# Routing in two groups of tokens, weights' low parts on VectorE, later weight requests and a shorter general path, in a fused attention and mixture-of-experts kernel

## The chip, the cores and the metric

One core of a Trainium2 chip runs the program. The metric is the device time of one execution in microseconds; the kernel before is quoted by the median of its runs. The trace comes from one further, profiled execution.

## The reference

```python
def _attn_ref(q, k, v):                      # 2 batches, 8 heads, 768 tokens, width 64
    gamma = 1.0 - 2.0 ** (-5.0 - np.arange(H, dtype=np.float32))
    for t in range(S):
        state = gamma[None, :, None, None] * state + np.einsum('bhd,bhe->bhde', k[:, :, t], v[:, :, t])
        y[:, :, t] = scale * np.einsum('bhd,bhde->bhe', q[:, :, t], state)
...
def _moe_ref(x, w_gate, w1, w2, capacity):   # 1536 tokens, 8 experts, 512 -> 1024 -> 512
    logits = x @ w_gate
    expert_idx = np.argmax(logits, axis=1)
...
    for i in range(N):                       # a token's place is its rank within its expert
        e = expert_idx[i]
        if counts[e] < capacity:
            disp[e, counts[e]] = x[i]
...
    h = np.maximum(np.einsum('ecd,edf->ecf', disp, w1), 0.0)
    y = np.einsum('ecf,efd->ecd', h, w2)
...
        out[i] = gate_w[i] * y[expert_idx[i], pos[i]]
...
def _moe2_ref(x, w_in, w_out, a, b):         # 512 -> 2048 -> 512
    h = x @ w_in
    P = a[0] + a[1] * h + a[2] * h2 + a[3] * h3
    Q = 1.0 + np.abs(b[0]) * np.abs(h) + np.abs(b[1]) * h2
    return (P / (Q + 1e-06) @ w_out).astype(np.float32)
```

The three parts run one behind the other. The capacity is 384 tokens for each expert.

## The kernel before, in words

**Attention and routing** (`attention`, L539 to L637). The 1,536 tokens are twelve tiles of 128, numbered u, six for each batch. For each tile TensorE makes the scores (`scores`, line 328 as all of `mm`), the product with the running state (`inter`), the product with the values (`intra`), the new state (`state`), and one product that turns the tile and gives the gate's logits (`gate_mm`, L345). VectorE masks the scores (`mask`, L292) and scales the result (`attn_xt`, L334). GpSimd scales the values (`scale`, L264) and makes the tables of decay (`y_table`, L259). ScalarE copies the state, the logits and the rows (`gate_out`, L393), which go to a table `xd` in HBM.

Tokens are routed in groups of whole tiles, `GROUPS`; before these are 4, 3, 3 and 2 tiles. For a group VectorE finds the expert of each token (`gate_group`, L373 to L384), TensorE ranks the tokens within their experts (`rank_mm`, L410 to L420), VectorE turns ranks into slots (`rank_pos`, L444 to L455, and `rank_put`, L465 to L468), and TensorE puts the tokens' numbers into a table of slots (`place_mm`, L478), which VectorE adds up (L483). From the table come the indices (`indices`, L496) by which GpSimd gathers rows of `xd` (`fetch`, L792).

**Weights.** All products of the experts use each weight as a high and a low part. A half matrix (128x1024) is requested on SP's queue (`load_w`, L157); ScalarE makes its high part `whi` (`split_hi`, L143), then the low part `wlo` is a subtraction (`split_lo`, L148). During attention the tables `LOADS`, `HI_AT` and `LO_AT` say at which tile a half is requested and split; there the low part is GpSimd's work. From the expert stage on, `prep_next` splits on ScalarE and VectorE and keeps loads ahead.

**The tail and the first expert** (`attn_tail`, L652; `first_expert`, L750). Of expert 0, the first 128 tokens are known once the first seven tiles are placed. Their rows are gathered early (`early_gather`), turned (L644), and run through expert 0 (L686 for the first layer, 24 products; L714 for the second, 24) while the last tiles are still routed. All other gathers wait for the last group's indices. The first of them feeds L842.

**Experts 1 to 7 and the last layer** (`moe` from L854, `ffn`). Each expert is a run of products (L871 to L873, L898 to L900), and SP, ScalarE, VectorE and GpSimd prepare the next weights beside it.

**The general path** (`overflow`, L918). Behind expert 3 every engine reads a flag (L920) and branches (L925). When an expert has more tokens than its slots, a loop redoes all experts in a plain way; on these inputs the branch skips it. Every engine jumps over its own part of that code.

The order of the instructions on each engine is the order in which the code issues them.

## Time and profile before

| | us |
|---|---|
| median of 3 runs (531.73 to 534.88) | 533.1 |
| the profiled execution, its own time | 539.45 |
| its span in the trace | 537.7 |
| TensorE matmul busy, of the span | 509.7 (95%) |
| TensorE instructions in the trace | 3,540 matmuls, 3,540 weight loads |
| VectorE busy, of the span | 416.2 (77%) |
| mean granted TensorE clock | 0.985 |

PE is TensorE, PEld its weight loads, DVE VectorE, ACT ScalarE, POOL GpSimd, SP the queue that issues most transfers. A `q` behind an engine's name means its sequencer. Times in the trace are microseconds from the start of the span. Matmuls are pipelined, so a busy PE is not PE at its peak.

### The profile page before, as it was taken

How to read it: one execution, taken by the hardware profiler on the slowest of the kernel's cores; microseconds unless marked ns; L12 is line 12 of the kernel's file. 1: busy time of each engine (PE TensorE's matmuls, PEld its weight loads, DVE VectorE, ACT ScalarE, POOL GpSimd, SP SyncE). 2: the span in 40 equal slices, each digit the busy share in tenths (PEclk: the TensorE clock that was granted, in tenths of full speed). 3: DMA queues.
4: the chain of work that ended last, by engine and by line, in shares of the span. 5: the costliest groups of instructions: out<-in, count | busy, mean ns of one | idle time of the engine just before them, and what ended most of it. 6: DMA issues, size and time to landing. Idle time of an engine off the chain costs nothing.

```text
span 537.7 us, 9505 instructions
## 1 busy us (share of the span) xinstructions
PE 509.7 (95%) x3540; PEld 446.1 (83%) x3540; DVE 416.2 (77%) x644; ACT 361.4 (67%) x591; POOL 261.5 (49%) x195
## 2 busy tenths in 40 slices
PE   6989889999995899999999999999999999999994
PEld 3877767899995899999988888888888888888883
DVE  2479973887967387798569698999899998865972
ACT  1334423886674277685578899998999988676750
POOL 1676503124826164212035444776757765535765
PEclk9999989999999699999999999999999999999998
DMA  8998554689998589997610001230222200000103
GB/s 307 411 395 320 144 172 149 210 321 258 286 315 255 162 291 217 371 280 272 218 37 2 0 1 39 80 111 17 69 79 79 78 1 0 2 0 1 79 2 156
DMA packets 27123, 83.16 MB, mean 155 GB/s; under 512 B 4928, under 2 KB 5184, under 8 KB 27072
## 3 DMA queue, kind: packets, MB, share of 16 engines
q1 hardware_dynamic: 24448, 75.16, 42.9%
q0 software_dynamic: 2624, 7.35, 4.0%
q8 instruction: 29, 0.48, 0.3%
q14 instruction: 22, 0.18, 0.1%
HBM read 72.00 MB, written 10.49 MB: 153 GB/s over the span
## 4 chain that ended last, share of the span: by engine, by line
PE 73%; issue 4%; DVE 3%; DMA 3%; ACT 2%; POOL 2%; POOLq 0%; ACTq 0%; DVEq 0%
PE h L997 8%; PE h L999 8%; PE h L998 8%; PE o L1068 7%; PE o L1070 7%; PE o L1069 7%; PE l L871 4%; PE l L872 4%; PE l L873 4%; PE l L900 4%; PE l L899 4%; PE l L898 4%; PE l L714 2%; DMA wd<-gq 2%; PE l L686 2%
## 5 line engine op out<-in xcount | busy, mean ns | idle before, releaser
L148 DVE TENSOR_TENSOR wlo<-raw,whi 128x1024 fp32r<-128x1024 f32 x72 | 101.6, 1425 | 16.7 <-ACT whi L143 16.4
L1048 POOL TENSOR_TENSOR gg<-fx,gg 128x512 fp32r<-128x512 f32 x47 | 61.0, 1298 | 70.7 <-issue 62.5
L143 ACT ACTIVATE whi<-raw 128x1024 fp32r<-128x1024 f32 x80 | 83.1, 1053 | 3.5 <-PE l L899 2.1
L997 PE MATMUL h<-yh,whi 128*128 128x512 f32 x192 | 74.9, 390 | 0.4 <-DVE fx L1036 0.4
L1068 PE MATMUL o<-whi,gg 128*128 128x512 f32 x192 | 74.8, 390 | 0.0
L999 PE MATMUL h<-yh,wlo 128*128 128x512 f32 x192 | 74.8, 389 | 0.0
L998 PE MATMUL h<-yl,whi 128*128 128x512 f32 x192 | 74.7, 389 | 0.0
L1069 PE MATMUL o<-wlo,gg 128*128 128x512 f32 x192 | 74.7, 389 | 0.0
L1070 PE MATMUL o<-whi,gg 128*128 128x512 f32 x192 | 74.7, 389 | 0.0
L1023 POOL TENSOR_TENSOR fw<-fh,fw 128x512 f32<-128x512 f32 x48 | 64.3, 1340 | 20.8 <-ACT fw L1012 20.1
L871 PE MATMUL l<-xh,whi 128*128 128x224 f32 x224 | 63.5, 283 | 7.5 <-issue 7.5
L204 POOL TENSOR_TENSOR gq<-gq 128x512 int32<-128x512 int32 x16 | 25.2, 1575 | 92.7 <-DVE gq L201 67.9
L1010 ACT ACTIVATE fx<-h,ct 128x512 f32<-128x512 f32 x48 | 37.3, 777 | 39.4 <-PE h L999 37.8
L872 PE MATMUL l<-xl,whi 128*128 128x224 f32 x224 | 62.9, 281 | 0.0
L873 PE MATMUL l<-xh,wlo 128*128 128x224 f32 x224 | 62.8, 280 | 0.0
L898 PE MATMUL l<-hh,whi 128*128 128x224 f32 x224 | 61.9, 276 | 0.0
L900 PE MATMUL l<-hh,wlo 128*128 128x224 f32 x224 | 61.5, 274 | 0.0
L899 PE MATMUL l<-hl,whi 128*128 128x224 f32 x224 | 61.4, 274 | 0.0
L871 PEld LDWEIGHTS l<-xh,whi 128*128 128x128 f32 x224 | 44.4, 198 | 7.7 <-issue 7.7
L872 PEld LDWEIGHTS l<-xl,whi 128*128 128x128 f32 x224 | 44.4, 198 | 0.0
L873 PEld LDWEIGHTS l<-xh,wlo 128*128 128x128 f32 x224 | 44.4, 198 | 0.0
L1034 DVE SCALAR_TENSOR_TENSOR fw<-fw,cq,h 128x512 f32<-128x512 f32 x48 | 35.6, 742 | 10.0 <-ACT h L1029 10.0
(167 smaller groups left out, 1233.1 us busy)
## 6 DMA issues: line engine op xcount, KB each, us to landing
raw<-wm SPq DMA_DIRECT2D x64, 512.0 KB
r<-wf SPq DMA_DIRECT2D x32, 512.0 KB
kv<-kv SPq DMA_DIRECT2D x24, 512.0 KB
wd<-gq SPq DMA_DIRECT2D x16, 256.0 KB
raw<-wd SPq DMA_DIRECT2D x8, 512.0 KB
xd<-xs SPq DMA_DIRECT2D x12, 256.0 KB
ca<-ct SPq DMA_DIRECT2D x1, 384.0 KB
xg<-xd,gidx POOLq DMA_INDIRECT x16
```

The costliest lines, as they stand in the source:

```text
L143: nc.scalar.activation(out=self.whi[i][:, sl], in_=raw, func=AF.Copy)
L148: (eng or self.nc.vector).tensor_tensor(out=self.wlo[i][:, sl], in0=raw, in1=self.whi[i][:, sl].bitcast(F32), op=ALU.subtract)
L871: nc.tensor.matmul(ps[:, fi], lhsT=wh[:, sl], rhs=xh[:, k], start=(k == 0), stop=False)
L872: nc.tensor.matmul(ps[:, fi], lhsT=wh[:, sl], rhs=xl[:, k], start=False, stop=False)
L873: nc.tensor.matmul(ps[:, fi], lhsT=wl[:, sl], rhs=xh[:, k], start=False, stop=(k == 3))
L898: mm(lhsT=wh[:, ws], rhs=fh, start=(f == 0 and o % 2 == 0), stop=False)
L997: nc.tensor.matmul(h, lhsT=wh[:, sl], rhs=self.yh[:, k, ts], start=(k == 0), stop=False)
L998: nc.tensor.matmul(h, lhsT=wh[:, sl], rhs=self.yl[:, k, ts], start=False, stop=False)
L999: nc.tensor.matmul(h, lhsT=wl[:, sl], rhs=self.yh[:, k, ts], start=False, stop=(k == 3))
L1068: self.nc.tensor.matmul(ps, lhsT=gh[:, ms], rhs=wh[:, ws], start=first, stop=False)
L1069: self.nc.tensor.matmul(ps, lhsT=gh[:, ms], rhs=wl[:, ws], start=False, stop=False)
L1070: self.nc.tensor.matmul(ps, lhsT=gl[:, ms], rhs=wh[:, ws], start=False, stop=last)
```

## The change

Eight things are changed together.

1. **Groups**: two groups, tiles 0 to 6 and 7 to 11, in place of four.
2. **Low parts in attention on VectorE**, at other tiles: halves 0 to 3 within the loop, 4 and 5 in the tail, 6 and 7 in `first_expert`. The high parts are issued behind the gate's copies, also later. `LOADS` requests weights later.
3. **Order in the tail**: the last `gate_mm` is issued first, then `early_x` and sixteen of the products that need no low part of x, then the ranking. `first_expert` takes the second layer's products with the high part first.
4. **Start**: the decay table `t0` comes with the first transfer; the values of tile 0 are scaled on GpSimd, those of tile 1 on VectorE; the matrix of ones is set on the chip.
5. **Pairs of PSUM banks**: the two halves of scores and of results are one tile each, so `mask` and `attn_xt` are one instruction for each tile. The heads are laid out so that this works.
6. **PSUM pools**: attention has its own.
7. **Scatter of the row numbers** (`perm_put`): experts 4 to 7 in place of 1 to 4.
8. **The general path** has 16 plain products and 12 turns in its inner loop in place of 40 and 4.

```diff
-GROUPS = (0, 4, 7, 10, 12)
+GROUPS = (0, 7, 12)
 DEC0 = 10
 LAG = (2, 3, 4, 5)
 WA, WC = 9, 3
-LOADS = (0, 1, 1, 1, 1, 1, 1, 1, 1, 1, 1, 1)
-HI_AT = {n + 3: (n,) for n in range(8)}
-LO_AT = {n + 4: (n,) for n in range(8)}
+LOADS = (0, 1, 0, 1, 0, 1, 0, 2, 1, 1, 1, 2)
+HI_AT = {5: (0,), 6: (1,), 9: (2,), 10: (3, 4), 11: (5,)}
+LO_AT = {6: (0,), 7: (1,), 10: (2,), 11: (3,)}
...
+    def pair_bank(self, tag, name):
+        return self.pm.tile([128, 1024], F32, tag=tag, name=name, bufs=1)
...
+        self.nc.vector.tensor_tensor(out=scm, in0=sc, in1=m, op=ALU.mult)
...
+        self.nc.vector.tensor_tensor(out=x, in0=yt, in1=qd, op=ALU.mult)
...
-            n0, n1 = self.cols["ident"][0], self.cols["t0"][0]
+            n0, n1 = self.cols["ident"][0], self.cols["tri"][0]
...
-            self.attn_load(0, 0)
             nc.sync.dma_start(out=self.ca[:, 0:n1], in_=a["ct"][:, 0:n1])
-            for u, c in ((0, 1), (1, 0), (1, 1)):
-                self.attn_load(u, c)
+            for u in range(2):
+                for c in range(2):
+                    self.attn_load(u, c)
+            nc.sync.dma_start(out=self.ct, in_=a["ct"][:, n0:])
+            for u in range(2, 4):
+                for c in range(2):
+                    self.attn_load(u, c)
             nc.sync.dma_start(out=self.ca[:, n1:], in_=a["ct"][:, n1:n0])
-            nc.sync.dma_start(out=self.ct, in_=a["ct"][:, n0:])
-            for u, c in ((2, 0), (2, 1), (3, 0), (3, 1)):
-                self.attn_load(u, c)
             dve, pool = nc.vector, nc.gpsimd
             dve.memset(self.wu, 0.0)
+            dve.memset(self.ones, 1.0)
             self.warm(WA)
             self.scores(0)
             self.mask(0)
-            self.scale(0, dve)
             self.y_table(0, pool)
-            self.scale(1, pool)
             self.y_table(1, pool)
+            self.scale(0, pool)
+            self.y_table(2, pool)
...
-                    self.split_lo(n // 2, n % 2, pool)
+                    self.split_lo(n // 2, n % 2)
...
+                    self.scale(1, dve)
...
-                for n in HI_AT.get(u, ()):
-                    self.split_hi(n // 2, n % 2)
-                if u:
-                    self.gate_mm(u - 1)
                 if u - 2 in done and not last:
                     self.rank_mm(done[u - 2])
                 if u:
+                    self.gate_mm(u - 1)
                     self.gate_out(u - 1, (0,))
                 if u - 1 in done:
                     self.gate_group(done[u - 1])
                 if u:
                     self.gate_out(u - 1, (1,))
+                for n in HI_AT.get(u, ()):
+                    self.split_hi(n // 2, n % 2)
...
         u, b = NU - 1, len(GROUPS) - 2
+        l1 = (*range(8), *range(12, 20), *range(8, 12), *range(20, 24))
+        self.gate_mm(u)
         self.early_x()
-        ps = [self.bank(t, "l1") for t in ("s1", "s0")]
-        self.rank_mm(b - 1)
-        self.win_l1(self.x0, ps, 0, 4)
-        self.rank_pos(b - 1)
-        self.early_lo()
-        self.gate_mm(u)
+        ps = self.pair_bank("s", "l1").rearrange("p (a n) -> p a n", a=2)
+        ps = [ps[:, 0], ps[:, 1]]
+        self.win_l1(self.x0, ps, l1[:16])
+        self.split_lo(2, 0)
         self.gate_group(b)
         self.gate_out(u)
-        self.rank_put(b - 1)
-        self.h0 = self.wp.tile([128, 2, 512], F32, tag="wt", name="h0", bufs=3)
-        self.win_l1(self.x0, ps, 4, 9)
+        self.early_lo()
+        for n in (6, 7):
+            self.split_hi(n // 2, n % 2)
+        self.load_next(4)
         self.rank_mm(b)
         self.rank_pos(b)
+        self.h0 = self.wp.tile([128, 2, 512], F32, tag="wt", name="h0", bufs=3)
+        self.win_l1(self.x0, ps, l1[16:20])
+        self.win_relu(ps, self.h0, 0)
         self.rank_put(b)
-        self.win_l1(self.x0, ps, 9, 13)
-        self.win_relu(ps, self.h0, 0)
-        self.place_mm(b - 1, "y1")
-        self.win_l1(self.x0, ps, 13, 18)
-        self.place_mm(b, "y1")
+        self.win_l1(self.x0, ps, l1[20:])
+        self.win_relu(ps, self.h0, 1)
+        tp = self.win_turn(self.h0, 0, self.bank("xk", "htp"))
+        self.place_mm(b, "lg")
+        self.split_lo(2, 1)
         self.indices(self.gidx, E * (self.nsub + 1))
+        self.ht0 = self.win_parts(tp)
         self.counts()
...
-        self.ht0 = self.win_split(self.h0, 0, self.bank("xk", "htp"))
-        self.win_l1(self.x0, ps, 18, 24)
-        self.win_relu(ps, self.h0, 1)
         self.nprep = 8
...
-        self.win_l2(self.ht0, acc, 0, 0, 6)
+        self.win_l2(self.ht0, acc, 0, (0, 1, 3, 4, 6, 7, 9, 10))
         ht1 = self.win_split(self.h0, 1, tp)
+        for half in range(2):
+            self.split_lo(3, half)
         self.rows()
-        self.win_l2(self.ht0, acc, 0, 6, 12)
+        self.win_l2(self.ht0, acc, 0, (2, 5, 8, 11))
         self.expert_x(0, 1)
...
-                    if 1 <= e < 5 and q < 3:
-                        self.perm_put(3 * (e - 1) + q)
-                    if (e, q) == (5, 3):
+                    if e >= 4 and q < 3:
+                        self.perm_put(3 * (e - 4) + q)
+                    if (e, q) == (7, 3):
                         self.perm_get()
...
                     w = [tmp(f"hl{k}") for k in range(4)]
                     for k in range(4):
                         nc.sync.dma_start(out=w[k], in_=wm[fh][:, k * 512 : k * 512 + 512])
-                    for f in range(4 * fh, 4 * fh + 4):
-                        ps = self.bank("l1", "ops")[:, 0:128]
-                        fs = slice(f % 4 * 128, f % 4 * 128 + 128)
-                        for k in range(4):
-                            nc.tensor.matmul(
-                                ps,
-                                lhsT=w[k][:, fs],
-                                rhs=xt[:, k * 128 : k * 128 + 128],
-                                start=(k == 0),
-                                stop=(k == 3),
-                            )
-                        nc.scalar.activation(out=hs[fh][:, fs], in_=ps, func=AF.Relu)
-                py = self.bank("l1", "opy")
-                for fh in range(2):
+                    ps = self.bank("l1", "ops")
+                    for k in range(4):
+                        ks = slice(k * 128, k * 128 + 128)
+                        nc.tensor.matmul(ps, lhsT=xt[:, ks], rhs=w[k], start=(k == 0), stop=(k == 3))
+                    nc.scalar.activation(out=h, in_=ps, func=AF.Relu)
+                    tp = self.bank("tp", "otp").rearrange("p (k n) -> p k n", k=4)
+                    for k in range(4):
+                        nc.tensor.transpose(tp[:, k], h[:, k * 128 : k * 128 + 128], self.col("ident"))
+                    nc.scalar.activation(out=ht, in_=tp.rearrange("p k n -> p (k n)"), func=AF.Copy)
                     w = [tmp(f"hl{k}") for k in range(4)]
                     for k in range(4):
                         nc.sync.dma_start(out=w[k], in_=wm[2 + fh][:, k * 512 : k * 512 + 512])
-                    for f in range(4 * fh, 4 * fh + 4):
-                        nc.tensor.matmul(
-                            py,
-                            lhsT=hs[fh][:, f % 4 * 128 : f % 4 * 128 + 128],
-                            rhs=w[f % 4],
-                            start=(f == 0),
-                            stop=(f == 7),
-                        )
+                    for k in range(4):
+                        ks = slice(k * 128, k * 128 + 128)
+                        first, last = fh == 0 and k == 0, fh == 1 and k == 3
+                        nc.tensor.matmul(py, lhsT=ht[:, ks], rhs=w[k], start=first, stop=last)
```

## Rows read from the trace of the kernel before

**Rows 1.** Stages: length, then each engine's busy us (instructions), granted clock, DMA share, GB/s.

```profile
4.96:18.03 13.07, 9.37 (x141) 7.91 (x140) 5.98 (x12) 2.15 (x9) 4.77 (x5) 1.00 0.99 392
...
37.24:48.16 10.92, 9.99 (x136) 8.66 (x136) 10.67 (x25) 3.54 (x9) 8.16 (x6) 1.00 1.00 368
48.16:63.38 15.22, 14.33 (x230) 12.61 (x229) 14.45 (x38) 6.51 (x19) 7.49 (x4) 1.00 0.62 201
...
84.32:100.63 16.31, 16.31 (x84) 12.38 (x85) 8.28 (x18) 9.82 (x15) 3.53 (x4) 1.00 0.34 102
```

**Rows 2.** Timeline of PE's weight loads, attention to first gather: start, us, instruction, [idle before].

```profile
18.03 0.97 PEld L328 LDWEIGHTS sc<-kv 64*128 64x128 f32 x16
...
22.33 0.97 PEld L328 LDWEIGHTS sc<-kv 64*128 64x128 f32 x16
...
37.24 0.29 PEld L328 LDWEIGHTS sc<-kv 64*128 64x128 f32 x2 [2.41 <-DVE scm L292]
...
68.28 0.42 PEld L644 LDWEIGHTS xtp<-ct,xg 128*128 128x128 f32 x4 [2.23 <-DMA xg<-xd,gidx]
...
76.10 0.74 PEld L478 LDWEIGHTS tp<-rr,pe 128*128 128x128 f32 x6 [0.72 <-DVE pe L468]
...
84.32 0.42 PEld L842 LDWEIGHTS tp<-ct,xg 128*128 128x128 f32 x4 [0.61 <-DMA xg<-xd,gidx]
```

**Rows 3.** Timeline of VectorE and GpSimd around the first group's routing.

```profile
33.70 2.35 POOL L148 TENSOR_TENSOR wlo<-raw,whi 128x1024 fp32r<-128x1024 f32 x1
33.71 2.39 DVE L381 TENSOR_TENSOR oh<-ct,m 128x32 bf16<-128x32 f32 x1
```

**Rows 4.** The low parts up to 100 us, both engines: ns min/median/max, first and last start.

```profile
L148 POOL TENSOR_TENSOR wlo<-raw,whi x8: 2349/2356/2372, 29.4 to 65.2; 128x1024 fp32r<-128x1024 f32 x8
L148 DVE TENSOR_TENSOR wlo<-raw,whi x3: 1224/1225/1226, 96.1 to 99.5; 128x1024 fp32r<-128x1024 f32 x3
```

**Rows 5.** Groups by form: VectorE up to 100 us, then ScalarE's high parts from the page.

```profile
L292 DVE TENSOR_TENSOR scm<-sc,ca 128x512 f32<-128x512 f32 x24 | 15.4, 682 | 12.8 <-PE sc L328 12.8
...
L468 DVE TENSOR_TENSOR pe<-ct,pm 128x512 f32<-128x512 f32 x1 | 0.7, 684 | 0.0
...
L143 ACT ACTIVATE whi<-raw 128x1024 fp32r<-128x1024 f32 x80 | 83.1, 1053 | 3.5 <-PE l L899 2.1
```

**Rows 6.** Timeline of the start, VectorE.

```profile
11.73 0.76 DVE L334 TENSOR_TENSOR xt<-yt,ca 128x256 f32<-128x256 f32 x2 [2.94 <-DMA ca<-ct]
```

**Rows 7.** The two stretches of half clock within the first 190 us (columns as Rows 1).

```profile
70.40:73.85 3.45, 3.45 (x14) 3.02 (x13) 2.28 (x13) 0.50 (x4) 0.00 (x0) 0.52 0.00 0
172.80:183.05 10.25, 6.30 (x29) 6.30 (x30) 0.22 (x1) 0.80 (x2) 0.00 (x0) 0.51 0.58 171
```

**Rows 8.** Timeline of the last indices and gather, VectorE and GpSimd.

```profile
79.39 0.18 DVE L496 TENSOR_SCALAR gidx<-tab 128x32 int32<-128x32 f32 x1
...
79.85 1.01 POOL L792 DMA_INDIRECT xg<-xd,gidx  x1 [12.27 <-DVE off L488]
```

**Rows 9.** The chain that ended last: start, us, what.

```profile
87.75 4.14 PE l L686 x18
```

**Rows 10.** The stages ahead of the stop and of the stop (columns as Rows 1).

```profile
166.00:169.30 3.30, 3.29 (x30) 3.10 (x28) 3.09 (x3) 0.95 (x2) 3.06 (x3) 1.00 1.03 413
169.30:176.75 7.45, 0.00 (x0) 0.00 (x0) 1.72 (x3) 1.65 (x3) 1.51 (x1) 0.74 0.54 91
```

**Rows 11.** PE's sequencer, line 925, then line 871 from 169 to 177 us.

```profile
L925 PEldq EVENT_SEMAPHORE  x1: 51/51/51, 169.3 to 169.3; - x1
...
L871 PEldq EVENT_SEMAPHORE  x1: 51/51/51, 169.5 to 169.5; - x1
```

**Rows 12.** PE's code queue: packets, MB, share; whole span, 174.4 to 176.75 us, 182.7 to 183.2.

```profile
q8 instruction: 29, 0.48, 0.3%
...
q8 instruction: 1, 0.02, 2.7%
...
q8 instruction: 1, 0.02, 12.1%
```

More of the change, by code (lines that the diff above doesn't have):

```diff
@@ L64, in table_layout @@
         ("tri", 128),
-        ("ones", 128),
         ("ident", 128),
@@ L280, in scores @@
         kt, qt = self.feats(u)
-        for r in range(2):
-            self.sc[u, r] = self.bank(f"s{r}", "sc").rearrange("p (j t) -> p j t", j=4)
+        sc = self.sc[u] = self.pair_bank("s", "sc").rearrange("p (r j t) -> p r j t", r=2, j=4)
         for j in range(4):
@@ L285, in scores @@
                 rows = slice(64 * r, 64 * r + 64)
-                self.mm(self.sc[u, r][:, j], kt[rows, j], qt[rows, j], True, True)
+                self.mm(sc[:, r, j], kt[rows, j], qt[rows, j], True, True)
     def mask(self, u):
-        m = self.col("mask").unsqueeze(1).to_broadcast([128, 4, 128])
-        scm = self.scm[u] = self.ap.tile([128, 2, 4, 128], F32, tag="scm", name="scm", bufs=2)
-        for r in range(2):
-            self.nc.vector.tensor_tensor(out=scm[:, r], in0=self.sc.pop((u, r)), in1=m, op=ALU.mult)
+        m = self.col("mask").unsqueeze(1).to_broadcast([128, 8, 128])
+        scm = self.scm[u] = self.ap.tile([128, 8, 128], F32, tag="scm", name="scm", bufs=2)
+        sc = self.sc.pop(u).rearrange("p r j t -> p (r j) t")
+        self.nc.vector.tensor_tensor(out=scm, in0=sc, in1=m, op=ALU.mult)
     def state(self, u):
@@ L308, in inter @@
     def inter(self, u):
-        self.yt[u] = [self.bank(f"y{r}", "yt")[:, 0:256].rearrange("p (k t) -> p k t", k=2) for r in range(2)]
+        y = self.pair_bank("y", "yt").rearrange("p (r n) -> p r n", r=2)
+        yt = self.yt[u] = y[:, :, 0:256].rearrange("p r (k t) -> p r k t", k=2)
         if u % UPB == 0:
@@ L331, in attn_xt @@
         xt = self.ap.tile([128, 4, 128], F32, tag="xt", name="xt", bufs=2)
[L332 to L336 removed]
+        x, qd = (t.rearrange("p (r k) t -> p r (k t)", r=2) for t in (xt, self.qd[u % UPB]))
+        yt = self.yt.pop(u).rearrange("p r k t -> p r (k t)")
+        self.nc.vector.tensor_tensor(out=x, in0=yt, in1=qd, op=ALU.mult)
         self.xt[u] = xt
@@ L697, in win_split, with win_turn @@
     def win_split(self, h, half, tp):
-        nc = self.nc
+        return self.win_parts(self.win_turn(h, half, tp))
+    def win_turn(self, h, half, tp):
         r = h.shape[0]
@@ L702, in win_split, with win_parts @@
             fs = slice(f * 128, f * 128 + 128)
-            nc.tensor.transpose(tp[:, f], h[:, half, fs], self.col("ident")[0:r, 0:r])
+            self.nc.tensor.transpose(tp[:, f], h[:, half, fs], self.col("ident")[0:r, 0:r])
+        return tp
+    def win_parts(self, tp):
+        nc, r = self.nc, tp.shape[2]
         ht = self.wp.tile([128, 2, 4, 128], F32R, tag="wt", name="ht", bufs=3)[:, :, :, 0:r]
@@ L707, in win_split, with win_l2 @@
         return ht
-    def win_l2(self, ht, acc, half, lo, hi):
-        for i in range(lo, hi):
+    def win_l2(self, ht, acc, half, seq):
+        for i in seq:
             f, r = divmod(i, 3)
@@ L1222, in shape_tables @@
     put("tri", np.triu(np.ones((128, 128)), 1))
-    put("ones", 1.0)
     ct = ct.astype(np.float32)
```

53 lines of the change are left out of this document (24 added, 29 removed).

## The prediction

> **What bounds the kernel now.** I read the table of stages first, then TensorE's idle gaps in the timeline, then the chain that ended last. From 84.32 us on TensorE is busy without a break (16.31 of 16.31 us up to expert 1 [rows 1]), and what follows is a run of products whose preparation lies beside it. So this change can move the end in two places alone: how early TensorE reaches the first product on gathered rows, L842 at 84.32 [rows 2], and whether it stops on the way. It stops once for long, behind the branch: no product from 169.30 to 176.75 [rows 10].
>
> Ahead of 84.32 TensorE is the pace, at 4.30 us a tile (18.03 to 22.33 [rows 2]), except where routing makes it wait: 2.41 us for a mask that stood behind the first group's routing on VectorE, 2.23 us for the early gather [rows 2]. VectorE is full there, 10.67 of 10.92 us and then 14.45 of 15.22 [rows 1], much of it lost to GpSimd: a result of 32 columns took 2.39 us while GpSimd's low part took 2.35 [rows 3].
>
> The sum is made against the profiled execution, 539.45 us (span 537.7). The median shown is 6.35 us lower; I carry the sum over unchanged.
>
> **The start.** The first transfer grows by 256 KB (t0's 512 columns), at 392 GB/s [rows 1] 0.7 us, so kv of tile 0 comes 0.8 us later. GpSimd scales tile 0's values in place of VectorE. In return the first result no longer waits 2.94 us for t0 [rows 6]. Through both chains tile 2's scores begin some 0.35 us later than before, at 13.9.
>
> **Attention.** Products are the same in number. The first group is routed at tile 7, not 4. Eight low parts leave GpSimd (2.36 us each); four come to VectorE within the loop, at 1.23 [rows 4]. One mask of 1024 columns for two of 0.68 [rows 5]: between 0.68 and 1.36, I take 1.2, and nothing at the end, since TensorE is the pace. The low part is issued ahead of the mask (tiles 6, 7, 10) or the result (tile 11), and waits for ScalarE's 1.05 us high part [rows 5], now behind the gate's copies. At tile 6 that ends VectorE's mask at 39.45 against 38.55 when TensorE wants the bank: 0.95 us of idle. At tiles 7 to 10 I find no wait: mask and result are 2.0 us, a low part 1.2, each of the three routing steps about 2 (13 small operations in 2.28 us [rows 7]), so VectorE needs some 5.2, 4.0 and 4.0 us in tiles 7, 8 and 9 of 4.3 each, and the lag of a tile between mask and use takes up the rest. So, with the 0.35: tile 6 at 34.95, tile 7 at 39.5, tile 8 at 43.8, tile 9 at 48.4 (an estimated 0.3 of ranking), tile 10 at 52.7, tile 11 at 58.75 (seven tiles placed are fourteen passes at 0.74/6 [rows 2], 1.75). Before, tile 11 began at 63.38, the edge between two stages [rows 1].
>
> **The tail.** Tile 11's result waits for low part 3 (high part to 60.5, low part to 61.75, result to 62.45), so the last gate product runs from 62.5 to 63.5, 1.25 us after TensorE was free. The early gather, released at 58.4, lands by 62.9 (4.47, as the gather below) and no longer counts. Turn and copy of x to 64.8; sixteen products at 0.23 (4.14 us for 18 [rows 9]) to 68.55; only then the ranking, whose inputs were ready near 66, to 69.35 (an estimated 0.8). VectorE: slots to 70.8, tables to 72.55 (five tiles: 640 columns at 684 ns for 512 [rows 5]); ten placing passes to 73.85, table 74.1. Then low part 5 stands ahead of the indices: 1.23, all of it on the path. Indices 75.55, GpSimd 75.85; from its start to L842 was 4.47 us (79.85 to 84.32 [rows 2, 8]), so L842 at 80.3: **-4.0**. Low parts 6 and 7 in first_expert lie beside that gather; if it came at once they would cost up to 2.5 of VectorE.
>
> TensorE has nothing to do for some 2.8 us of that gather. [...]
>
> Requests for weights come later, but each half still at least three tiles (12 us) ahead of its split; 0, unless SP stands behind a late row copy. Moving perm_put and perm_get costs 0: experts 1 to 7 have GpSimd idle, and perm is read at the end alone; if GpSimd were late there, three scatters' microseconds. Pools and the ones matrix: 0.
>
> **The branch.** Behind the branch TensorE's sequencer got through an event at 169.3 and the first one of line 871 at 169.5; the product behind it started at 176.75, with nothing that it waited for [rows 10, 11]. Its code queue moved no block from 169.4 until one at 174.4, and 2.3 us after that TensorE ran; the next block came at 182.7, 6.0 us after [rows 12]. 29 blocks [rows 12] for 7,080 matmuls and loads are about 250 instructions each. I read: the jump landed on the last instructions of a block, and the following block is asked for only on entry. So TensorE waited out the fetch: 5.0 us to its start, 2.35 to running. With the half clock behind it (6.30 us busy at 0.51 [rows 7], 3.15 lost) the branch cost 7.45 + 3.15 = 10.6.
>
> The general path is shorter by 80 TensorE instructions: a plain product is four (eight calls, sixteen weight loads [rows 2], as many matmuls), a turn two (L842, four calls, x4), so 40*4 + 4*2 = 168 become 16*4 + 12*2 = 88. Product counts ahead of the branch don't change (ranking 24 and 24, placing 12). The landing moves 80 instructions back from the block's end, which is 40 products at 0.11 us (30 in 3.30 us [rows 10]), 4.4 us of work while the fetch runs. The stall falls from 7.35 to 2.9, with ends 0 (a quicker fetch) and 4.0 (6.0 + 2.35 - 4.4). Behind 2.9 us idle I take the shorter stretch again, 1.7, with ends 0 and 5.1. **-10.6 + 2.9 + 1.7 = -6.0**.
>
> Sum: -4.0 + 1.7 - 6.0 = -8.3: 531.2 for the profiled execution, **524.8** for the median.
>
> [...]
>
> **Rivals.** (1) The fetch is wholly covered: 80 instructions suffice and no clock is lost. For it, the jump itself cost nothing (169.3 to 169.5); against, 4.4 is less than 7.35. -2.3 - 10.6: 520.2. (2) The stall stays: any taken branch flushes PE's code, wherever it lands. The two events before it speak against. -2.3 alone: 530.8. (3) VectorE becomes the bound of attention: its 25.1 us from 37.24 to 63.38 [rows 1] stay stretched by GpSimd's scaling and four low parts, 4.9, come on top: 30.0 against 26.1 elapsed, tile 11 at 63.38 - 2.4 + 3.9 = 64.9, L842 as long after it as above (21.55) at 86.45, +2.1, clock +1.7, branch -6.0: 530.9. (4) Slower: TensorE's clock. The new order breaks the tail into gaps of 0.6 to 2.8 us; if half clock lasts as long as the 10.25 us stretch each time, the tail's 7.3 us of products on the path double (+7.3), expert 0 behind the gather loses 5.1, and the branch keeps 5.1 in place of 1.7: -4.0 + 7.3 + 5.1 - 2.6 = +5.8, 538.9. It decides once half clock holds from 64 through the ranking. Before, gaps of 0.72 and 0.61 behind 74 brought none [rows 2].
>
> **How the numbers follow.** Forecast 0.50, rivals in order 0.20, 0.12, 0.12, 0.06. 0.5% (2.7 us) is about what a measurement of this kernel can tell from no change, so faster means below 530.4. Forecast and rival 1 count as faster, with a third of rivals 2 and 3, which lie just above that line: 0.78. Same 0.15, slower 0.07. The range takes in rival 1 with a tail shorter by another 2.7 us (517.5) and rivals 2 and 3 with 0.6 more (531.5). The forecast's own range is 520.2 to 528.6: from both clock stretches gone and 1.2 off the tail, to the 4.0 us stall with 2.7 more in the tail.
>
> **What would show it.** Start: the first result without a wait for ca; tile 2's scores near 13.9. Attention: tile 11 near 58.8, no mask wait near 37, one near 39 behind a low part. Tail: low part 5 directly ahead of the indices, L842 near 80.3 after a gap of 2 to 3 us, granted clock below 1 behind it. Branch: about 40 products between line 925's event and a stop of about 3 us, with one code block landing within it. Wrong would be: a stop of 7 us at once, VectorE without idle while TensorE waits for masks from tile 7 on, or L842 behind 84.

## The result and the profile after

The change makes the kernel 1.7% faster: **525.19 us** (median of 6 runs, 523.24 to 525.90) against 533.75 us (6 runs, 531.73 to 536.49) on the same chip; ratio 0.9833, 95% interval 0.9801 to 0.9866. That is 8.56 us less; the forecast was 8.3 less, 524.8 us. The sum came out, but not by the steps of the prediction: part of the gain comes from a move that it priced at zero, and some of its errors cancel, as the experiments show. Ratios here and below leave out runs that took over 1.5% longer than the fastest of the same kernel beside them; that takes five of 13 runs from the kernel before beside short_path and pad80 (those of 538.16 us and more), and none elsewhere.

The profiled execution took 524.94 us (span 523.2, mean granted clock 0.994, before 0.985). Against the profile of before that is 14.5 us, not 8.6: the execution shown of before was 5.70 us above its median of six runs, with a long stop behind the branch.

The timeline of TensorE's products in the changed kernel (start, us, instruction, [idle before]), from tile 7 to the first product on gathered rows and the low-part wait behind it (tiles counted by the turns of the attention loop, as in the prediction):

```profile
38.74 1.16 PE L330 MATMUL sc<-kv 64*128 64x128 f32 x16 [1.01 <-DVE scm L293]
...
47.88 1.16 PE L330 MATMUL sc<-kv 64*128 64x128 f32 x16 [0.29 <-DVE scm L293]
...
61.83 1.17 PE L344 MATMUL xk<-wi,xt 128*128 128x136 f32 x8 [0.97 <-DVE xt L336]
...
75.75 0.47 PE L722 MATMUL l<-whi,ht 128*128 128x512 f32 x1 [2.31 <-DVE off L486]
...
80.63 0.60 PE L852 MATMUL tp<-ct,xg 128*128 128x128 f32 x4
...
82.13 0.50 PE L722 MATMUL l<-wlo,ht 128*128 128x512 f32 x1 [0.66 <-DVE wlo L147]
```

The mask wait of 2.41 us at 37.24 and the 2.23 us for the early gather [rows 2] are gone. In their place stand a wait of 1.0 for a mask at tile 7, 0.3 at tile 9 (the expectations below say tile 10), 0.97 ahead of tile 11's gate products, and a gap of 2.3 us at 75.75. L852, which was L842 at 84.32 [rows 2], comes at 80.63 and waits for nothing. Behind it there is a wait of 0.66 us that the prediction did not have.

VectorE in the same stretch shows what the masks and the result stand behind:

```profile
35.78 1.78 DVE L147 TENSOR_TENSOR wlo<-raw,whi 128x1024 fp32r<-128x1024 f32 x1 [2.08 <-ACT whi L142]
...
59.86 1.22 DVE L147 TENSOR_TENSOR wlo<-raw,whi 128x1024 fp32r<-128x1024 f32 x1 [2.28 <-ACT whi L142]
...
73.62 1.22 DVE L147 TENSOR_TENSOR wlo<-raw,whi 128x1024 fp32r<-128x1024 f32 x1
74.75 0.17 DVE L495 TENSOR_SCALAR gidx<-tab 128x32 int32<-128x32 f32 x1
...
75.44 0.17 DVE L486 COPY off<-rk 128x16 f32<-128x16 f32 x1
...
80.86 2.35 DVE L147 TENSOR_TENSOR wlo<-raw,whi 128x1024 fp32r<-128x1024 f32 x2
```

Low parts 0 and 3 hold VectorE idle for 2.08 and 2.28 us while their high part is made, with a mask or a result queued behind them. Low part 5 stands directly ahead of the indices. The copy of the counts (L486) stands behind it and ht0's low part, and the gap of 2.3 us on TensorE ends with this copy. That gap is not the gather's: it began at 73.44, and GpSimd started the gather only at 75.20:

```profile
75.20 1.00 POOL L802 DMA_INDIRECT xg<-xd,gidx  x1 [16.14 <-DVE gidx L495]
```

Low parts 6 and 7 come only at 80.86, behind ht1's low part: that is the new wait on TensorE at 82.13.

Three rows of TensorE make a ruler for the rest, the first products of experts 1, 3 and 5 in the changed kernel, then those of 3 and 5 before:

```profile
97.79 0.27 PE L881 MATMUL l<-xh,whi 128*128 128x224 f32 x1
...
142.75 0.28 PE L881 MATMUL l<-xh,whi 128*128 128x224 f32 x1
...
187.75 0.27 PE L881 MATMUL l<-xh,whi 128*128 128x224 f32 x1
```

```profile
145.59 0.28 PE L871 MATMUL l<-xh,whi 128*128 128x224 f32 x1
...
202.21 0.27 PE L871 MATMUL l<-xh,whi 128*128 128x224 f32 x1
```

From expert 3's first product to expert 5's (the branch lies between) the changed kernel takes 45.00 us, the kernel before 56.62. An expert without a branch takes 22.3 (120.45 to 142.75), so 44.6 would be no stop at all. From expert 5's first product to the end of the span it is 335.4 in one and 335.5 in the other. So the 14.5 us of the two profiles are 2.84 up to expert 1 (100.63 [rows 1] to 97.79) and 11.62 behind the branch, and nothing else. "The branch stretch" below is this 45.00 or 56.62.

Behind the branch the changed kernel hardly stops:

```profile
165.37 0.34 PE L881 MATMUL l<-xh,whi 128*128 128x224 f32 x1 [0.15 <-PEq L935]
```

### The profile page after: what moved, and what is told of

It is laid out like the page before. It is cut to its first block, busy times and chain, and to the rows that moved or that the text cites. A ratio compares the mean times of both kernels' runs of the same rounds, so it can differ in the third digit from the quotient of the medians.

```text
span 523.2 us, 9413 instructions
## 1 busy us (share of the span) xinstructions
PE 504.5 (96%) x3540; PEld 441.5 (84%) x3540; DVE 405.9 (78%) x576; ACT 361.7 (69%) x588; POOL 244.2 (47%) x187
## 4 chain that ended last, share of the span: by engine, by line
PE 62%; issue 2%; POOL 1%; ACT 1%; DVE 1%; POOLq 0%; ACTq 0%
PE h L999 8%; PE h L1000 8%; PE h L1001 8%; PE o L1071 7%; PE o L1070 7%; PE o L1072 7%; PE l L881 3%; PE l L883 3%; PE l L882 3%; PE l L910 3%; PE l L909 3%; PE l L908 3%; POOL out L1101 1%; PE tp L852 1%; ACT fh L1030 0%
## 5 line engine op out<-in xcount | busy, mean ns | idle before, releaser
L147 DVE TENSOR_TENSOR wlo<-raw,whi 128x1024 fp32r<-128x1024 f32 x80 | 112.3, 1418 | 20.0 <-ACT whi L142 19.7
L1025 POOL TENSOR_TENSOR fw<-fh,fw 128x512 f32<-128x512 f32 x48 | 64.2, 1338 | 15.3 <-ACT fw L1014 14.5
L881 PE MATMUL l<-xh,whi 128*128 128x224 f32 x224 | 62.0, 277 | 0.2 <-PEq L935 0.2
L883 PE MATMUL l<-xh,wlo 128*128 128x224 f32 x224 | 61.5, 275 | 0.0
L882 PE MATMUL l<-xl,whi 128*128 128x224 f32 x224 | 61.4, 274 | 0.0
L881 PEld LDWEIGHTS l<-xh,whi 128*128 128x128 f32 x224 | 43.0, 192 | 0.4 <-ACT yh L745 0.3
L909 PEld LDWEIGHTS l<-hl,whi 128*128 128x128 f32 x224 | 43.0, 192 | 0.1
L908 PEld LDWEIGHTS l<-hh,whi 128*128 128x128 f32 x224 | 43.0, 192 | 0.1
```

What stands on the lines that cost most here:

```text
L147: (eng or self.nc.vector).tensor_tensor(out=self.wlo[i][:, sl], in0=raw, in1=self.whi[i][:, sl].bitcast(F32), op=ALU.subtract)
L881: nc.tensor.matmul(ps[:, fi], lhsT=wh[:, sl], rhs=xh[:, k], start=(k == 0), stop=False)
L883: nc.tensor.matmul(ps[:, fi], lhsT=wl[:, sl], rhs=xh[:, k], start=False, stop=(k == 3))
L908: mm(lhsT=wh[:, ws], rhs=fh, start=(f == 0 and o % 2 == 0), stop=False)
L909: mm(lhsT=wh[:, ws], rhs=fo, start=False, stop=False)
```

## The experiments

They ran on three chips, so medians are compared on one chip, or as ratios to the kernel before on that chip, where the medians of all its runs were 533.7 to 537.9 us. Its runs scattered from 529.6 to 541.9; those of the changed kernel kept within 523.1 to 525.9.

| kernel | median us (runs) | ratio to before, interval | branch stretch us |
|---|---|---|---|
| before, again | 535.12 (1) | | 50.23 |
| short_path | 532.97 (10) | 0.9980, 0.9935 to 1.0025 | 51.55 |
| perm_only | 533.27 (10) | 0.9905, 0.9871 to 0.9938 | 50.04 |
| short_perm | 527.37 (4) | 0.9858, 0.9786 to 0.9930 | 45.00 |
| after, again | 523.68 (4) | 0.9786, 0.9715 to 0.9856 | 45.00 |
| perm_back | 530.26 (4) | 0.9892, 0.9819 to 0.9966 | 49.73 |
| pad80 | 529.71 (4) | 0.9885, 0.9796 to 0.9974 | 51.15 |
| pad120 | 530.19 (1) | | 50.20 |
| lo_after | 522.05 (4) | 0.9753, 0.9685 to 0.9822 | 45.00 |
| pool_lo | 523.69 (4) | 0.9760, 0.9689 to 0.9831 | 45.00 |
| tail2 | 523.85 (4) | 0.9779, 0.9707 to 0.9850 | 44.99 |
| best3 | 520.14 (6) | 0.9698, 0.9645 to 0.9751 | 45.00 |

**1. The kernel before, again**, on the chip of the next three.

> The kernel before, unchanged, in another profiled execution. Theory A (the stop behind the branch is the wait for a code block that is asked for on landing, and its length depends on how long that fetch takes): TensorE again stops at the first product of expert 4, by somewhere between 2.5 and 8 us, with half clock behind a long stop; the span differs from 537.7 us by about what the stop and the half clock differ. Theory B (the stop is a fixed price of a taken branch): 7.5 us again, within 0.5. The traced run of before was 5.7 us over its median, so A expects a shorter stop here, near 4 us.

The stop behind the branch is half as long as in the execution on which the prediction rests:

```profile
PE l L871 <- issue: 3.7, 1, 3.7
```

(That is the view of waits: who waited for what, us in total, times, the longest.) The 7.45 us of [rows 10] were a long case. This execution lost its time elsewhere, to half clock in the attention stage (last section).

**2. The shorter path alone**, in the kernel before:

```diff
-                    for f in range(4 * fh, 4 * fh + 4):
-                        ps = self.bank("l1", "ops")[:, 0:128]
-                        ... 16 products of 128 columns, then 16 of 512 as before
+                    ps = self.bank("l1", "ops")
+                    for k in range(4):
+                        nc.tensor.matmul(ps, lhsT=xt[:, ks], rhs=w[k], start=(k == 0), stop=(k == 3))
+                    ... four transposes, four products
```

> The kernel before with the shorter general path alone. Its landing lies 82 TensorE instructions ahead of the end of a code block, in place of 1. Theory A: no stop over 1 us behind the branch, no half clock there, and 4 to 7 us less than before in the timed runs (0.987 to 0.993). Theory B (any taken branch pays): the stop stays, ratio 1.000. Theory C (all of the gain lies in attention and tail): ratio 1.000 as well, but without a stop in either.

A miss by the ratio: 0.998, with an interval that takes in 1. Against the median of all 13 runs of the kernel before there (537.32) it is 4.35 us lower, so the medians alone leave the size open. The trace decides more: the branch stretch is 51.55, not 45. TensorE did run through its landing (first product behind it at 167.60, branch at 165.91), but it stopped 8 us later, for ScalarE:

```profile
179.41 0.90 PE L842 MATMUL tp<-ct,xg 128*128 128x128 f32 x3 [3.53 <-ACT xg L832]
```

and ScalarE had been standing for 4 us:

```profile
171.23 0.64 ACT L193 ACTIVATE gq<-r 128x512 int32<-128x512 uint32 x1
175.87 0.54 ACT L876 ACTIVATE hh<-l 128x448 fp32r<-128x448 f32 x1 [4.01 <-PE l L873]
```

The view puts the 4.01 down to the products of L873, yet the first group of these (24 at 0.11 us from 167.60) was through by about 170.3. SP, which issues the transfers, had jumped at 167.78 and did nothing until 175.5; VectorE waited for ScalarE's output. One code packet of 8 KB for these engines, from 167.80 on, took 4.69 us, where the other four of that stretch took 0.31 to 0.56. That points to a stop that had moved from TensorE's code to that of the others; experiments 5 to 7 test it.

**3. The landing moved back to where it was**, in the changed kernel: eleven times as many turns in one loop of the path that is not run (80 TensorE instructions more in it), and **4.** 120 more.

```diff
-                    for k in range(4):
+                    for k in [*range(4)] * 11:
```

> The kernel after with 40 more turns in the skipped loop, 80 TensorE instructions, so that the landing lies 2 instructions ahead of the end of a code block, as in before; nothing that is executed differs. Theory A: the stop is back, 2.5 to 8 us at the first product of expert 4, and the time is 529 to 533 us, against 525 for after (ratio to before 0.991 to 0.998). Theory B: no change against after by the landing, 525 us. Theory C: 525 us.

> The kernel after with 60 more turns in the skipped loop, 120 instructions: the landing lies 38 instructions into the block behind the one that pad80 lands in. Theory A: that block was not asked for ahead of the jump, so TensorE stops before its first event behind the branch, by as much as in pad80, and doesn't stop again at a block's end. If the code that is at hand reaches further than one block, there is no stop. Theory B: the same as in after.

The path isn't run. Both stop again; their waits are, first pad80, then pad120,

```profile
PE l L882 <- issue: 3.0, 1, 3.0
```

```profile
PE l L881 <- PEq L935: 3.7, 1, 3.7
```

and in pad120 it is the branch instruction itself that takes the time, 5.11 us where it takes 0.35 in the changed kernel:

```profile
L935 PEldq COMPARE_BRANCH  x1: 5112/5112/5112, 163.7 to 163.7; - x1
```

Nothing that runs differs, only where the jump lands. In the branch stretch it costs 6.2 and 5.2 us: the stop of 3.0 or 3.7 and half clock behind it (6.83 us at 0.50 in pad80, columns as Rows 1). The medians say 4.5 us or more, on different chips (529.71 against 525.19 and 523.68).

```profile
166.92:173.75 6.83, 6.19 (x29) 6.19 (x30) 0.32 (x1) 0.90 (x2) 0.00 (x0) 0.50 0.80 256
```

So the three landings cost 0.15 us with 82 instructions left in the block (after), 3.0 with 2 left (pad80: TensorE ran one product, a load and a matmul, and stopped), and 5.11 in the branch itself for a landing in the next block (pad120). The counts are the author's; the 82 are seen in experiment 5, in the 41 products that ran ahead of a stop. When a block is asked for, no trace shows, only when its packet moves.

**5. The scatters of the permutation back in experts 1 to 4**, in the changed kernel. The prediction had costed this move at 0.

```diff
-                    if e >= 4 and q < 3:
-                        self.perm_put(3 * (e - 4) + q)
-                    if (e, q) == (7, 3):
+                    if 1 <= e < 5 and q < 3:
+                        self.perm_put(3 * (e - 1) + q)
+                    if (e, q) == (5, 3):
```

It ran with the changed kernel itself and with **6.**, the reverse: the kernel before with the shorter path and the scatters moved.

> The changed kernel unchanged, on the chip of the next three. 524 to 526 us; first product of expert 1 at 97.8 us of the span, 45.0 us from expert 3's first product to expert 5's (the stretch with the branch; two experts are 44.6), 335.4 from there to the end. If the code fetches behind the branch are a matter of luck and not of the kernel, that stretch is 50 in some profile of this kernel.

> The changed kernel with the twelve scatters of the permutation back in experts 1 to 4, so that the last ones run beside the branch, as before. Theory S (the scatters' 128 small packets each slow the code fetches of SP, ACT and DVE behind the branch, which took 0.9 to 4.7 us in the kernels with scatters there and 0.3 to 0.5 in those without): expert 3's first product to expert 5's grows from 45.0 to 49 to 52 us, 529 to 532 us in all. Theory C (only where PE's landing stands in its code counts, the scatters are free as predicted): 45.0 to 45.6 us, 524.5 to 526.5 us in all.

> The kernel before with the shorter general path and the scatters moved to experts 4 to 7, nothing else. The shorter path alone left expert 3's first product to expert 5's at 51.6 us (533.0 us in all). Theory S: 45 to 47 us, 527 to 529 us in all. Theory C: 51 to 52 us again (the wait moves from PE's fetch to ACT's, whatever the scatters do), 532 to 534 us.

Theory S held in both directions. The changed kernel, run again, took 523.68 us with a branch stretch of 45.00; its expert 1 came at 96.00, not 97.8, since it had no half clock in the tail. With the scatters back it is 6.58 us slower on this chip (530.26, with no run of the one in the range of the other). Of this the branch stretch shows 4.73 (49.73 against 45.00). In the two profiles another 2.16 us lie ahead of expert 1, where no scatter has run yet and perm_back had half clock for 6.83 us; so 4.7 us is what the traces give to the scatters. The kernel before gains 6.37 us by the two moves together (533.74 to 527.37), and in short_perm TensorE lands without a stop:

```profile
165.42 0.34 PE L871 MATMUL l<-xh,whi 128*128 128x224 f32 x1 [0.15 <-PEq L925]
```

In perm_back TensorE ran on for 41 products and stopped. That is 82 instructions, a load and a matmul each, just what the expectation of short_path counts from the landing to the end of its block:

```profile
173.39 0.45 PE L883 MATMUL l<-xh,wlo 128*128 128x224 f32 x1 [2.71 <-issue]
```

The DMA view of the 4 us behind each landing (queue, packets, MB, share of 16 engines; q8 is read as TensorE's code and q14 as that of other engines, by what they moved in the kernel before, 0.48 and 0.18 MB, where 7,080 of the 9,505 instructions in the trace are TensorE's; q0 carries the scatters, q1 the bulk transfers), first of perm_back, then of the changed kernel (after, again):

```profile
q1 hardware_dynamic: 154, 0.56, 90.5%
q0 software_dynamic: 34, 0.00, 0.6%
q14 instruction: 1, 0.01, 0.5%
```

```profile
q1 hardware_dynamic: 112, 0.39, 24.9%
q14 instruction: 3, 0.02, 1.7%
q8 instruction: 1, 0.02, 1.5%
```

With scatters under way 0.56 MB of bulk keeps the DMA engines 90.5% busy; without them 0.39 MB takes 24.9%, so a bulk packet lasts 0.38 us (0.905 * 16 * 4.0 / 154) instead of 0.14. Less code gets through as well: one packet against four. Counted from the start of TensorE's branch instruction, its next code block started 2.8 to 3.0 us later in all ten profiles without scatters there, and 1.6, 3.0, 6.7 (the execution of the prediction) and 6.8 us (perm_back) later in the four with them. The same window gives bulk transfers 78 to 91% in the three other profiles with scatters there and 24.6 and 29.2% in short_perm and perm_only. The scatters' own packets are few and short (0.6%); that they are what slows the others is shown by moving them, not how.

**7. The fourth case**: the kernel before with the scatters moved and the long path kept (the diff of 5 reversed).

> The kernel before with the scatters moved to experts 4 to 7 and the long general path kept: the fourth of the four cases (shorter path alone 533.0 us, both 527.4). Theory B (two separate stops behind the branch, each enough to hold PE: PE's own fetch where it lands at the end of a block, and the slow fetches of the other engines beside the scatters; taking away one alone shows nothing): expert 3's first product to expert 5's at 50 to 51.5 us, a wait of PE of about 3 us at its first products behind the branch and half clock behind it, 531 to 534 us in all, no product of the stop above 4 us. Theory S alone (the scatters are the whole cause, PE's landing costs nothing): 45 to 46 us, 527 to 528.5 us in all. An additive pair would be 48 us and 530 us.

The stop stays, at 3.5 us, with a branch stretch of 50.04:

```profile
PE l L871 <- issue: 3.5, 1, 3.5
```

So there are two separate stops, and the branch stretch is 45.0 only with both gone: 50.2 and 56.6 with neither, 51.6 and 50.0 with one, 45.0 with both. By medians the scatters alone do help (ratio 0.9905, 4.66 us below the 537.93 of the kernel before on that chip), and against all runs the shorter path alone has 4.35. So "taking away one alone shows nothing" holds for these traces and went too far for the medians. One reason can be that the stop of the kernel before varies (7.45 and 3.7 us in its two profiles), so that one trace doesn't stand for its median. No intermediate of 48 us was seen in a trace, but the medians don't exclude that the two add.

**8. The low parts of the attention stage behind the result**, not ahead of the next mask, in the changed kernel:

```diff
-                for n in LO_AT.get(u, ()):
-                    self.split_lo(n // 2, n % 2)
...
                 self.attn_xt(u)
+                for n in LO_AT.get(u, ()):
+                    self.split_lo(n // 2, n % 2)
```

> The changed kernel with the four low parts of the attention stage issued behind the tile's gated product on VectorE, not ahead of the next tile's mask. Theory Q (the mask and the last gated product wait in VectorE's order behind a low part that itself waits for ScalarE): the waits of 1.0 to 1.2 us at tile 7, 0.3 at tile 10 and 0.97 ahead of tile 11's gate products go, expert 1's first product comes at 95.3 to 96.2 instead of 97.8 us, 522.7 to 524 us in all. Rival (VectorE is full, so the low part pushes the next mask or gated product as far): less than 0.7 us gained, 524.5 to 526 us.

Theory Q held. The mask waits are gone, and ahead of tile 11's gate products 0.55 us of another wait is left:

```profile
59.64 1.19 PE L344 MATMUL xk<-wi,xt 128*128 128x136 f32 x8 [0.55 <-ACT xs L392]
```

Expert 1's first product comes at 94.36 instead of 96.00 in the changed kernel on the same chip, 1.64 us, and the median is 1.63 us lower (521.52 to 523.12 against 523.10 to 525.19). Here a low part that waits for ScalarE cost TensorE nothing behind the work that it wants, and a wait ahead of it.

**9. The same low parts on GpSimd**, where they stood before, in the tiles of the change (`self.split_lo(n // 2, n % 2, pool)`).

> The changed kernel with the four low parts of the attention stage back on GpSimd, in the same tiles. Theory Q (on VectorE they stand ahead of masks and of the last gated product and cost 1.0 to 1.2 us at tile 7, 0.3 at tile 10, 0.97 ahead of tile 11's gate products): these waits go, and expert 1's first product comes 1 to 2 us earlier than in the changed kernel (94 to 96.5 us of the span), 522 to 524 us in all: the move to VectorE as made was a loss. Rival G (2.35 us on GpSimd instead of 1.22 on VectorE delays the scaling two tiles ahead and slows VectorE's masks beside it): the same or up to 2 us later, 524.5 to 527 us.

By the total neither is shown: 523.69 us, where the changed kernel has 523.68 on another chip. In the attention stage theory Q held: from tile 2's scores to tile 11's gate products it is 47.51 us (13.50 to 61.01), in the changed kernel 48.91 and 48.62 in its two profiles, in lo_after 47.13. The waits of tile 7 and of low part 3 go, one at tile 9 grows from 0.29 to 0.39, and on GpSimd each low part takes 2.36 us. That expert 1 came only at 97.18 has other reasons: this execution began tile 2 some 0.6 to 0.8 us later, with the same order of work up to there, and had one half-clock stretch in the tail.

```profile
36.61 2.36 POOL L147 TENSOR_TENSOR wlo<-raw,whi 128x1024 fp32r<-128x1024 f32 x1
...
47.48 1.16 PE L330 MATMUL sc<-kv 64*128 64x128 f32 x16 [0.39 <-DVE scm L293]
```

So the move to VectorE, as it was made, cost 1.1 to 1.4 us in this stage; put behind the result, the low parts cost no more on VectorE than on GpSimd (47.13 against 47.51).

**10. Three moves in the tail** of the changed kernel:

```diff
-        self.win_l1(self.x0, ps, l1[:16])
+        self.win_l1(self.x0, ps, l1[:5])
...
-        self.win_l1(self.x0, ps, l1[16:20])
+        self.win_l1(self.x0, ps, l1[5:20])
...
-        self.split_lo(2, 1)
         self.indices(self.gidx, E * (self.nsub + 1))
+        self.split_lo(2, 1)
         self.ht0 = self.win_parts(tp)
         self.counts()
+        for half in range(2):
+            self.split_lo(3, half)
...
-        for half in range(2):
-            self.split_lo(3, half)
```

> The changed kernel with three moves in the tail: the ranking behind five of the first-layer products, not sixteen; the indices ahead of low part 5; low parts 6 and 7 behind the counts, not behind ht1's low part. Theory R (GpSimd's indices, and with them the gather, hang on the ranking that waits 2.9 us in PE's order behind products, and on 1.2 us of low part 5): indices 3 to 4 us earlier against the gate products of tile 11, the first gathered product 2 to 3 us earlier, no wait of 0.5 to 0.7 us for low parts 6 and 7; expert 1's first product at 93 to 95 us, 520.5 to 522.5 us in all. Rival (the half of the products that follows the ranking now is what place waits for, or the gather's 4.5 us is not what PE waits for): less than 1 us gained.

Theory R fell, the rival held. The ranking did come 2.6 us sooner and the tables were ready at 68.95, but the placing products stand behind all 24 first-layer products in TensorE's order, and VectorE waited for them:

```profile
71.56 1.23 PE L477 MATMUL tp<-rr,pe 128*128 128x64 f32 x10
...
79.15 0.66 PE L852 MATMUL tp<-ct,xg 128*128 128x128 f32 x4 [0.48 <-DMA xg<-xd,gidx]
```

```profile
72.83 0.22 DVE L482 TENSOR_TENSOR tab<-tab,tp 128x64 f32<-128x64 f32 x1 [3.88 <-PE tp L477]
```

The indices came 1.1 us sooner without low part 5 ahead of them (73.08 against 74.21), yet the first gathered product did not (79.15; the changed kernel on another chip 78.94): from GpSimd's start of the gather to that product it was 5.6 us here, 4.3 there and 3.8 in the next kernel, where TensorE didn't wait for it. Of the difference 0.73 us is GpSimd's own instruction, 1.73 us here and 1.00 in the other two:

```profile
73.54 1.73 POOL L802 DMA_INDIRECT xg<-xd,gidx  x1 [15.24 <-DVE gidx L495]
```

What slows it, and the rest, stays open. The wait for low parts 6 and 7 went, as expected: expert 1 starts 16.29 us behind L852, not 17.06.

**11. The best of these together**, with the counts' copy ahead of the table's sum and ht0's low part ahead of low part 5, so that the second PSUM pool opens sooner (shown against tail2):

```diff
-        nc.vector.tensor_copy(self.off, self.cnt)
...
         self.rank_put(b)
+        self.nc.vector.tensor_copy(self.off, self.cnt)
...
-        self.split_lo(2, 1)
         self.ht0 = self.win_parts(tp)
+        self.split_lo(2, 1)
```

> lo_after and the three moves of tail2 together, with the counts' copy taken from PSUM ahead of the table's sum and ht0's low part ahead of low part 5, so that the second pool of PSUM opens 1.5 us sooner. Theories Q and R add up: expert 1's first product at 90.5 to 92.5 us, 517.5 to 519.5 us in all. If the gather's landing is now what PE waits for alone, the PSUM part adds nothing and it ends at 519 to 520.5 us.

520.14 us (519.95 to 520.35), ratio 0.9698: the fastest of all, within the second of the two ranges expected, though not for its reason: no wait for the gather is left. Expert 1's first product came at 93.02, later than the 90.5 to 92.5 expected. The gap ahead of the first product of the second layer (L722, here L724) shrank from 2.3 to 1.2 us, and all six runs had a granted clock of 0.996 to 0.998:

```profile
73.19 0.47 PE L724 MATMUL l<-whi,ht 128*128 128x512 f32 x1 [1.22 <-DVE ht L716]
...
76.48 0.60 PE L852 MATMUL tp<-ct,xg 128*128 128x128 f32 x4
```

## Why the prediction was right, and where it was not

For the profiled execution the prediction said 531.2 us, and it took 524.94; for the median it said 524.8, and 525.19 came. That the median agrees is in part luck: the execution from which the sum was made was 5.7 us over its median, with the longer of the two stops seen behind the branch, and the forecast left 4.6 us of stop and half clock there, where the changed kernel has next to none.

**The branch, -6.0: right in size, wrong in what makes it.** The medians of one chip give -6.4 for the shorter path and the moved scatters together. That TensorE landed at the end of a block and waited out the fetch was right, and the shorter path takes that stop away (0.15 us in the changed kernel; 3.0 and 3.7 with the landing moved back, pad80 and pad120). Three steps failed.
- "Moving perm_put and perm_get costs 0" is the largest: moved back, the scatters cost 4.7 us of the branch stretch. The step looked at who is idle and who reads perm, not at what the scatters do to other packets. The code queue that moved nothing until 174.4 is likely a trace of it, and was read as the branch's own latency: so late a block was seen in two of four profiles with scatters there and in none of ten without.
- "5.0 to its start, 2.35 to running" took the slow fetch for the normal one. The 2.35 held: 2.2 to 2.5 us from the block's start to the product in the five other stops. The 5.0 did not: in the changed kernel the next code block came 1.3 us after the landing (a packet of TensorE's code at 166.56, while it ran on), so 4.4 us of products covered it wholly. That is rival 1's mechanism; its 520.2 takes the whole of the long stop off the median. Left were neither the 2.9 us stop nor the 1.7 of half clock.
- The 7.45 us stop was the long one of two. The shorter one, 3.7 (before, again), plus 1.7 of half clock makes 5.4, near the 5.2 that its branch stretch is above 45.0. Two errors met: too large a stop before, too much left after.

**The tail, -4.0: the place came out, two waits on the way did not.** L842 from 84.32 to 80.63, forecast 80.3. Of its steps: tile 7 at 39.5 was 38.74 and its wait 0.95 was 1.0; tile 11's gate products at 62.5 were 61.83 behind a wait of 0.97 (forecast 1.25); indices at 75.55 were 74.75, GpSimd 75.85 was 75.20. From there on it went otherwise. The prediction let L842 wait for the gather behind 2.8 us of idle, and put the 1.7 us of half clock behind it. In the trace the 2.3 us of idle belong to the counts' copy, and L852 came 5.4 us behind GpSimd's start, rather than 4.47, because TensorE had products of its own until then, at half clock. In the changed kernel's second profile, without half clock, L852 came at 78.94, 5.4 us sooner than before, and the gather held it for 0.27 us only:

```profile
78.94 0.66 PE L852 MATMUL tp<-ct,xg 128*128 128x128 f32 x4 [0.27 <-DMA xg<-xd,gidx]
```

So 80.63 is near 80.3 by luck. Tail and clock together were forecast at -2.3; up to expert 1 they measured -2.84 in the profile shown and -4.63 in the second (100.63 to 97.79 and to 96.00). Low part 5 ahead of the indices was there, but "all of it on the path" failed, since TensorE's own products left the gather so little to hold. "Low parts 6 and 7 in first_expert lie beside that gather", priced at nothing there, failed too: 0.66 us of wait, and 17.16 us from L852 to expert 1 instead of 16.31.

**The start, +0.35: wrong in sign.** Tile 2's scores were forecast at 13.9 and came at 12.92 (TensorE's weight loads), since the first result came without the wait for t0 [rows 6] at 10.08, 1.65 us sooner, and kv of tile 0 was 0.44 us later (5.40 against 4.96), not 0.8. It is most of the 0.7 us by which the steps above are early.

**The clock, +1.7: one stretch was there, its sign over all runs was not.** The 1.7, here and again in the branch's sum, stands for a stretch like the shorter one of [rows 7], 3.45 us at 0.52. That a gap of 2.8 us brings one was the author's estimate, and no run shows it as a rule: in the trace of before a gap of 2.23 us was followed by half clock and one of 2.41 by none. The profile shown has half clock for 3.4 us in the tail, ahead of L852 and not behind the gather:

```profile
70.00:80.00 10.00, 7.05 (x32) 5.86 (x33) 4.62 (x18) 2.06 (x4) 3.88 (x4) 0.84 0.33 109
```

but the changed kernel's second profile has none behind the same gap of 2.3 us. And the kernel before loses more to it than its first profile showed, as the last section tells; short_perm, which keeps that kernel's attention, took 525.08, 526.79, 527.95 and 529.33 us at granted clocks of 0.997, 0.991, 0.988 and 0.982, while the changed kernel on that chip had 0.993 to 0.997.

**The low parts, 0 apart from the waits at tile 7 and tile 11: nearly right.** These two waits were there (1.0 and 0.97 us), and lo_after takes 1.64 us back. That VectorE loses time beside GpSimd's low part, as the prediction reads [rows 3], the trace of before shows by the same line: 0.17 to 0.18 us in the three other groups (16 or 24 columns), with no low part on GpSimd at that time. "At tiles 7 to 10 I find no wait" failed by 0.29 us: the mask that TensorE waited for stood behind the first routing step, which took VectorE 3.3 us (43.37 to 46.65) instead of 2. Rival 3 (VectorE the bound) and rival 4 (the clock, slower) did not occur; rival 2 (any jump flushes) fell with short_perm and the changed kernel, which jump with a wait of 0.15 us.

Routing in two groups was not tried alone. What is left for it with the other parts, against short_perm on the same chip, is 523.68 to 527.37, 3.7 us. The two profiles, both without half clock, show 1.8 of it (spans 523.3 and 521.5) as order of the work; the rest goes with the clocks just named.

## What to carry to other kernels

A move that is "off the path" is to be costed on the DMA queues too: list the packets that other engines will need in those microseconds, code blocks among them, and look whether small scatters share the time (beside the branch they cost 4.7 us here). Where all engines jump at once, a stop can have several owners; taking one away showed next to nothing in these traces until the last was gone (a branch stretch of 51.6 or 50.0 us with one, 45.0 with both), so undo parts from the fast side (from the changed kernel back) as well as from the slow one. An operation that waits for another engine belongs behind the work that the bound engine wants next (1.64 us here, lo_after).

## What the runs showed of the hardware that was not expected

**Scatters and code.** Beside the scatters, packets of the bulk queue took 0.38 instead of 0.14 us on average, and code blocks came late: TensorE's by 4 us in two of four profiles, and SP resumed 9.1 us behind its jump in perm_back (164.56 to 173.68) and 4.1 in the changed kernel (after, again; 161.53 to 165.64). The expectation of perm_back speaks of 128 small packets for each scatter; the trace of before has 32 (96 on q0 for three scatters from 204 to 212 us, 0.00 MB).

**Half clock in attention.** After the waits for masks behind the routing on VectorE, at 37 us, the kernel before ran at a granted clock of 0.50 in three of five profiles of it and its variants. The same stage of the kernel before (second profile) and after; columns as Rows 1:

```profile
38.20:45.00 6.80, 6.80 (x55) 6.26 (x56) 6.26 (x20) 1.40 (x3) 3.68 (x4) 0.50 1.00 375
```

```profile
38.20:45.00 6.80, 6.25 (x108) 5.47 (x110) 6.28 (x8) 2.27 (x7) 1.99 (x2) 1.00 1.03 392
```

55 products against 108 in 6.8 us. Ahead of it TensorE had been idle for 0.71 and 0.95 us within 2 us; the 2.41 us gap of [rows 2] was followed by none. In none of nine profiles of the changed kernel and its variants was the clock low in this stage, and the changed kernel's runs spread over 2.8 us where those of before spread over 12; that the clock makes this difference is likely, not shown. What makes the clock fall after one gap and not after another stays open.
